# Attention and rational FFN in fp32 halves: P times V head by head, with V high and V low side by side in the stationary tile

## The chip, the cores and the metric

The kernel runs on one core of one Trainium2 chip. The metric is the device time of one execution in microseconds (us); lower is better. The core has a matrix engine (TensorE, PE in the profile; PEld is its loading of stationary tiles), three engines for elementwise work (VectorE or DVE, ScalarE or ACT, GpSimd or POOL) and a queue from which all DMAs here are issued (SyncE or SP). PE writes to PSUM, eight banks of 128 partitions by 512 fp32 columns; POOL does not read PSUM in this kernel.

## The reference

Block-causal attention over 8 batches and 8 heads of 576 positions by 64, and then a feed-forward net (FFN) on the 4608 tokens, whose nonlinearity is a rational function:

```python
scores = scale * np.matmul(q, k.transpose(0, 1, 3, 2))
mask = (pos[:, None] // 64) >= (pos[None, :] // 64)
scores = np.where(mask, scores, -1000000000.0)
attn = np.exp(scores - np.max(scores, axis=-1, keepdims=True))
attn = attn / (np.sum(attn, axis=-1, keepdims=True) + 1e-09)
x = np.matmul(attn, v)          # then heads side by side: (4608, 512)
...
h = x @ w_in                    # (4608, 2048)
P = a[0] + a[1] * h + a[2] * h**2 + a[3] * h**3
Q = 1.0 + np.abs(b[0]) * np.abs(h) + np.abs(b[1]) * h**2
return (P / (Q + 1e-06)) @ w_out   # (4608, 512)
```

## The kernel before, in words

**Halves.** Matmuls run on fp32r operands. Each fp32 operand x is split into a high part (a cast to fp32r) and a low part (x minus the high part). A product is the sum of three matmuls: low times high, high times high, high times low.

**Attention.** The work goes by pairs of heads: 32 pairs (8 batches by 4), each called p. `load` brings Q, K and V in by DMA. `prep` transposes Q and K on PE into a PSUM bank (L410); ACT writes the high part (L414) and DVE the low part (L417); DMAs then lay high and low parts of one head below each other in 128 partitions. `scores` goes over five query tiles t (64, 128, 128, 128, 128 queries; 64 to 576 keys) and two heads j: two matmuls (L509, L510), a row maximum on DVE (L517, L521), exp with row sums on ACT (L525), normalisation on POOL (L539, L545), transposes of P on PE (L566), and again a high part on ACT (L581) and a low part on DVE (L583). Transposed P lies in `pt0`, `pt1`, `pt2`, one set for all pairs.

**P times V.** `vprep` splits V into `vpad`: per head and for the first block apart, four ACT casts (L453) and four POOL subtractions (L455). `vpad` holds the two heads' columns in such places, among zeros, that a 128-column window (`vblock`) gives an output with head 0 in partitions 0 to 63 and head 1 in 64 to 127, where one head's keys meet zeros of the other. `pv(p, g)` has two groups: g = 0 for the first three query tiles (5 key blocks, up to 320 columns) and g = 1 for the last two (9 blocks, 256 columns). Each block takes three matmuls (L604), so 15 and 27 per pair; all sum up in one bank. ACT writes the high part of the result (L617), DVE the low part (L619), and a DMA stores both in `xscr` (L622). The transposes of a pair wait for P times V of the pair before.

**FFN.** Chunks of 256 tokens (18 of them). Early units (`ffn0`: four units of two 128-wide columns of `w_in`, chunks 0 to 14) run beside attention: 24 matmuls of 256 columns (L741), the nonlinearity `wide` on ACT, POOL and DVE (L678 to L703), 12 matmuls of 512 columns (L760). All else is late (`ffn1`, chunks of 512 tokens, L855 and L881, 12 and 12 matmuls of 512 columns per unit; L858 where only one half of a chunk is left): 84 units. It starts when attention has given its memory back (`switch`).

**Order.** The kernel records every step as an operation with an engine, a modelled cost, a priority and its dependencies. `Plan.order` then goes through a modelled time: whenever an engine is free it takes the ready operation of the lowest `pri`, binds buffers and banks, and adds a LATENCY of the consuming engine to each dependency. What it gives out is the program order; each engine runs its queue in that order and waits on semaphores. Pools of empty slots are quotas on the eight banks: QA (6) for attention, QH (2) for the early FFN's h, QO (2) for its output.

## Time and profile before

| | before |
|---|---|
| median of 3 runs (lowest to highest) | 1280.77 us (1278.71 to 1282.59) |
| the profiled execution | 1278.76 us |
| its span, first to last instruction | 1276.6 us |
| busy: PE, PEld, DVE, ACT, POOL | 96%, 85%, 74%, 70%, 66% |
| P times V, first and last start (L604) | 29.8 and 792.5 us |
| first early FFN matmul (L741), first late one (L855) | 101.6 and 803.7 us |

In the slices of the page each digit is the busy share of a fortieth of the span, in tenths. A group's row gives its line, engine and operation, out<-in by name, the shape and the count, then the busy time in us, the mean in ns of one, and the idle time of the engine just before with what ended it. Matmuls overlap: a single one of 256 columns is shown 0.28 us long, while the next starts 0.12 us later, so stretches of the chain give their price better than their own length. In the rows of the waits stand who waited for whom, the sum in us, how often, and the longest.

### The profile page before, as it was taken

How to read it: one execution, taken by the hardware profiler on the slowest of the kernel's cores; microseconds unless marked ns; L12 is line 12 of the kernel's file. 1: busy time of each engine (PE TensorE's matmuls, PEld its weight loads, DVE VectorE, ACT ScalarE, POOL GpSimd, SP SyncE). 2: the span in 40 equal slices, each digit the busy share in tenths (PEclk: the TensorE clock that was granted, in tenths of full speed). 3: DMA queues.
4: the chain of work that ended last, by engine and by line, in shares of the span. 5: the costliest groups of instructions: out<-in, count | busy, mean ns of one | idle time of the engine just before them, and what ended most of it. 6: DMA issues, size and time to landing. Idle time of an engine off the chain costs nothing.

```text
span 1276.6 us, 23262 instructions
## 1 busy us (share of the span) xinstructions
PE 1230.6 (96%) x7560; PEld 1088.4 (85%) x7560; DVE 942.3 (74%) x1916; ACT 891.4 (70%) x2230; POOL 848.5 (66%) x1218
## 2 busy tenths in 40 slices
PE   7879999999999999999999999999999999999997
PEld 5669799899998999999988999888888888888885
DVE  7867887778787777778876876666676777677664
ACT  6778787778877788787787886555655555555554
POOL 6757876767767767676767776566665666665564
PEclk8989999999999999999999999999999999999999
DMA  5888876678777857786696741911142233224110
GB/s 147 217 235 213 221 191 174 179 191 210 192 194 185 225 162 200 180 212 187 165 236 181 196 133 63 379 47 41 59 132 67 89 109 118 81 66 132 34 33 33
DMA packets 222615, 195.12 MB, mean 153 GB/s; under 512 B 129312, under 2 KB 183584, under 8 KB 222496
## 3 DMA queue, kind: packets, MB, share of 16 engines
q1 hardware_dynamic: 222496, 193.65, 55.5%
q8 instruction: 60, 0.98, 0.3%
q14 instruction: 59, 0.48, 0.1%
HBM read 95.95 MB, written 44.56 MB: 110 GB/s over the span
## 4 chain that ended last, share of the span: by engine, by line
PE 68%; DVE 7%; DMA 7%; ACT 7%; POOL 6%; issue 3%; SPq 1%; POOLq 0%; ACTq 0%; DVEq 0%
PE psd L855 4%; PE psf L855 4%; PE psb L881 4%; PE psh L881 4%; PE pse L881 3%; PE psg L881 3%; PE psf L604 3%; DMA osa<-in_moe_w_in_dram 3%; PE psc L881 2%; PE psa L881 2%; PE psa L855 2%; PE psc L855 2%; PE psc L760 2%; PE psg L855 1%; PE psa L741 1%
## 5 line engine op out<-in xcount | busy, mean ns | idle before, releaser
L681 POOL TENSOR_SCALAR va<-ub,bab 128x512 f32<-128x512 f32 x60 | 46.8, 780 | 93.0 <-ACT ub L678 91.1
L681 POOL TENSOR_SCALAR vb<-ua,bab 128x512 f32<-128x512 f32 x57 | 44.2, 776 | 91.8 <-ACT ua L678 91.7
L703 POOL TENSOR_TENSOR glb<-sa,ghb 128x512 fp32r<-128x512 f32 x58 | 75.5, 1302 | 20.1 <-ACT ghb L702 17.7
L683 POOL TENSOR_TENSOR ub<-va,ub 128x512 f32<-128x512 f32 x60 | 77.9, 1299 | 4.6
L703 POOL TENSOR_TENSOR gla<-sb,gha 128x512 fp32r<-128x512 f32 x58 | 75.6, 1303 | 7.8 <-ACT gha L702 7.7
L455 POOL TENSOR_TENSOR vpl<-vra,vph 128x256 fp32r<-128x256 f32 (+1 forms) x128 | 67.8, 539 | 19.5 <-ACT vph L453 11.6
L683 POOL TENSOR_TENSOR ua<-vb,ua 128x512 f32<-128x512 f32 x57 | 74.0, 1298 | 4.6
L689 ACT ACTIVATE va<-ub,qcb 128x512 f32<-128x512 f32 x60 | 43.6, 727 | 46.0 <-POOL ub L683 45.8
L689 ACT ACTIVATE vb<-ua,qcb 128x512 f32<-128x512 f32 x57 | 41.3, 724 | 43.0 <-POOL ua L683 43.0
L702 ACT CAST ghb<-sa 128x512 fp32r<-128x512 f32 x58 | 36.1, 622 | 26.8 <-DVE sa L699 26.7
L702 ACT CAST gha<-sb 128x512 fp32r<-128x512 f32 x58 | 36.2, 624 | 11.1 <-DVE sb L699 10.9
L453 ACT CAST vph<-vra 128x256 fp32r<-128x256 f32 (+1 forms) x128 | 39.1, 324 | 1.8 <-POOL vph L323 0.4
L695 DVE SCALAR_TENSOR_TENSOR ub<-ub,psf 128x512 f32<-128x512 f32 x23 | 15.8, 686 | 25.5 <-ACT psf L693 25.4
L695 DVE SCALAR_TENSOR_TENSOR ub<-ub,psd 128x512 f32<-128x512 f32 x21 | 14.4, 687 | 26.5 <-ACT psd L693 26.3
L741 PE MATMUL psa<-x,wiha 128*128 128x256 f32 x176 | 33.2, 288 | 0.5 <-DVE sb L699 0.4
L741 PE MATMUL psf<-x,wiha 128*128 128x256 f32 x176 | 32.8, 285 | 0.5 <-DMA x<-xscr 0.5
L678 ACT ACTIVATE ua<-psf 128x512 f32<-128x512 f32 x25 | 15.0, 598 | 25.3 <-PE psf L855 21.1
L678 ACT ACTIVATE ua<-psd 128x512 f32<-128x512 f32 x24 | 14.3, 598 | 21.7 <-PE psd L855 19.4
L703 POOL TENSOR_TENSOR glb<-sb,ghb 128x512 fp32r<-128x512 f32 x14 | 18.1, 1296 | 16.1 <-ACT ghb L702 16.1
L741 PEld LDWEIGHTS psa<-x,wiha 128*128 128x128 f32 x176 | 27.3, 191 | 1.1 <-DVE sb L699 0.6
L741 PEld LDWEIGHTS psf<-x,wiha 128*128 128x128 f32 x176 | 27.5, 191 | 0.7 <-DMA x<-xscr 0.7
L741 PE MATMUL psb<-x,wiha 128*128 128x256 f32 x144 | 27.0, 286 | 0.0
(1662 smaller groups left out, 5599.0 us busy)
## 6 DMA issues: line engine op xcount, KB each, us to landing
xscr<-xsa SPq DMA_DIRECT2D x32, 320.0 KB, 2.9
x<-xscr SPq DMA_DIRECT2D x40, 256.0 KB, 4.5
qra<-in_q_dram SPq DMA_DIRECT2D x64, 144.0 KB, 3.7
qra<-in_k_dram SPq DMA_DIRECT2D x60, 144.0 KB, 2.9
vra<-in_v_dram SPq DMA_DIRECT2D x64, 128.0 KB, 2.5
xscr<-xsa SPq DMA_DIRECT2D x32, 256.0 KB, 3.7
ppa<-pscr SPq DMA_DIRECT2D x15, 512.0 KB, 4.0
osa<-in_moe_w_in_dram SPq DMA_DIRECT2D x10, 512.0 KB, 5.2
```

What stands on the lines that cost most here:

```text
L453: aop("ACT", (0.833 * n + 110, 0.833 * n + 200), lambda vh=vh, src=src: nc.scalar.copy(out=vh, in_=src()), rd=rd, wr=[("v", i, 0)], pri=pr ...
L455: aop("POOL", pool(n, True), lambda vh=vh, vl=vl, src=src: nc.gpsimd.tensor_tensor(out=vl, in0=src(), in1=vh.bitcast(F32), op=ALU.subtract ...
L604: nc.tensor.matmul(bank.t[:, s0:w], lhsT=vblock(vv, x), rhs=pp, start=(x == 0 and i == 0), stop=(x == nb - 1 and i == 2))
L681: op("POOL", pool(512, False, 2), lambda: nc.gpsimd.tensor_scalar(out=vt.t, in0=ut.t, scalar1=b1, scalar2=b0, op0=ALU.mult, op1=ALU.add), ...
L683: op("POOL", pool(512, True), lambda: nc.gpsimd.tensor_tensor(out=ut.t, in0=vt.t, in1=ut.t, op=ALU.mult), rd=[vt], wr=[ut], pri=pri)
L689: op("ACT", act(512, False, 1), lambda: nc.scalar.activation(out=vt.t, in_=ut.t, func=AF.Ln, bias=qcb), rd=[ut, "qcb"], wr=[vt], pri=pri)
L695: op("DVE", dve(512), lambda: nc.vector.scalar_tensor_tensor(out=ut.t, in0=ut.t, scalar=QC, in1=r0.t, op0=ALU.add, op1=ALU.mult), rd=rk, w ...
L702: op("ACT", act(512, False), lambda: nc.scalar.copy(out=gh.t, in_=st.t), rd=[st], wr=[gh], pri=pri)
L703: op("POOL", pool(512, True), lambda: nc.gpsimd.tensor_tensor(out=gl.t, in0=st.t, in1=gh.t.bitcast(F32), op=ALU.subtract), rd=[st, gh], wr ...
L741: nc.tensor.matmul(h.t[:, j * CT:(j + 1) * CT], lhsT=w[:, dc, fs], rhs=xb[dc // 2].t[:, dc % 2, hl, :], start=(dc == 0 and i == 0), stop=( ...
L855: nc.tensor.matmul(h.t, lhsT=w[:, dc, fs], rhs=x.t[:, dc, hl, :], start=(dc == 0 and i == 0), stop=(dc == 3 and i == 2))
L881: nc.tensor.matmul(o[m].t, lhsT=g.t[:, c0:c0 + 128], rhs=w[:, ff, :], start=(a and i == 0 and j == 0), stop=(z and i == 2))
```

## The change

**P times V.** V's split tile is now `VP`, 10 blocks of 128 columns: in each, V high in columns 0 to 63 and V low in 64 to 127. The first key block of the two heads has a block each (0 and 9), with zeros in the other 64 partitions, which the loaded tile brings along: it is filled with zeros there once, and the two small V loads go to blocks 0 and 9. `vprep` splits everything with one ACT cast and one POOL subtraction of 640 columns.

`pv` goes head by head. For head j it takes block 0 (or 9) and every second block after it, two matmuls each (P low and P high against the same stationary tile). The bank then has the product with V high in partitions 0 to 63 and that with V low in 64 to 127. ACT copies the lower part out to the head's 64 partitions of a new tile `xf`, DVE adds the upper part to it. When both heads are there, ACT casts `xf` to the high part and POOL (before: DVE) subtracts the low one. In group 0 each head has its own bank, in group 1 both share one.

**Order.** LATENCY is 90 for PE (250) and 80 for ACT (40); ACT and DVE work on attention's banks has 2 taken off its priority number (15); QH is 3 (2); scores and prep leave 2 banks of the quota free (1); loads come 9 earlier in priority, `vprep` 3 later; `gate` lets early FFN and weight loads 20 ahead (12); the split of the late weights begins at 90 (110); early FFN covers chunks 0 to 13, and chunk 14 goes to the late part, which then has 88 units.

```diff
-LATENCY = {"PE": 250, "ACT": 40,
+LATENCY = {"PE": 90, "ACT": 80,
...
-            o.pri -= 15
+            o.pri -= 2
...
-    QA, QH, QO, QH1, QO1, QR1, QR = (Pool([None] * n) for n in (6, 2, 2, 2, 4, 2, 1))
+    QA, QH, QO, QH1, QO1, QR1, QR = (Pool([None] * n) for n in (6, 3, 2, 2, 4, 2, 1))
...
-    def gate(pri, ahead=12):
+    def gate(pri, ahead=20):
...
-        pri = 10 * p - 12 + 0
+        pri = 10 * p - 12 + -9
...
-        pri = 10 * p + 3
...
+        pri = 10 * p + 6
+        vp = s["vp"] = Buf(VP)
+        aop("ACT", (0.833 * 640 + 110, 0.833 * 640 + 200), lambda: nc.scalar.copy(out=vp.t[:, :, 0:D], in_=vr.t),
+            rd=[(vr, j, i) for j in range(2) for i in range(2)], wr=[(vp, 0)], pri=pri)
+        aop("POOL", pool(640, True), lambda: nc.gpsimd.tensor_tensor(
+            out=vp.t[:, :, D:2 * D], in0=vr.t, in1=vp.t[:, :, 0:D].bitcast(F32), op=ALU.subtract),
...
-                for i, (vv, pp) in enumerate(((vh, lo), (vh, hi), (vl, hi))):
-                    nc.tensor.matmul(bank.t[:, s0:w], lhsT=vblock(vv, x), rhs=pp,
-                                     start=(x == 0 and i == 0), stop=(x == nb - 1 and i == 2))
...
+        xf = Buf(XF)
+        whole = Buf(banks, QA) if g else None
+        for j in range(2):
+            bank, at = (whole, 256 * j) if g else (Buf(banks, QA), 0)
...
+                xs_ = (0, *range(1 + j, nb, 2))
...
+                    for i, pp in enumerate((lo, hi)):
+                        nc.tensor.matmul(bank.t[:, at + s0:at + w], lhsT=vp.t[:, x or 9 * j], rhs=pp,
+                                         start=(x == 0 and i == 0), stop=(x == xs_[-1] and i == 1))
...
+            aop("ACT", act(w), lambda bank=bank, at=at, j=j: nc.scalar.copy(
+                out=xf.t[64 * j:64 * j + 64, :w], in_=bank.t[64:128, at:at + w]), rd=[(bank, j)], wr=[(xf, j)], pri=pri)
+            aop("DVE", dve(w), lambda bank=bank, at=at, j=j: nc.vector.tensor_tensor(
+                out=xf.t[64 * j:64 * j + 64, :w], in0=bank.t[0:64, at:at + w], in1=xf.t[64 * j:64 * j + 64, :w],
+                op=ALU.add), rd=[(bank, j)], wr=[(xf, j)], pri=pri)
...
-        aop("ACT", act(w), lambda: nc.scalar.copy(out=xs.t[:, 0, :w], in_=bank.t[:, :w]),
-            rd=[bank], wr=[(xs, 0)], pri=pri)
-        aop("DVE", dve(w), lambda: nc.vector.tensor_tensor(
-            out=xs.t[:, 1, :w], in0=bank.t[:, :w], in1=xs.t[:, 0, :w].bitcast(F32), op=ALU.subtract),
+        aop("ACT", act(w, False), lambda: nc.scalar.copy(out=xs.t[:, 0, :w], in_=xf.t[:, :w]),
+            rd=[(xf, 0), (xf, 1)], wr=[(xs, 0)], pri=pri)
+        aop("POOL", pool(w, True), lambda: nc.gpsimd.tensor_tensor(
+            out=xs.t[:, 1, :w], in0=xf.t[:, :w], in1=xs.t[:, 0, :w].bitcast(F32), op=ALU.subtract),
...
-    split_weights(wscr, NFA, NFB, [110 + 220 * i / NPLB for i in range(NPLB)], True)
+    split_weights(wscr, NFA, NFB, [90 + 220 * i / NPLB for i in range(NPLB)], True)
...
-    U0 = [list(range(EARLY[c] if c < len(EARLY) else 4 if c < NCH - 3 else 0)) for c in range(NCH)]
+    U0 = [list(range(EARLY[c] if c < len(EARLY) else 4 if c < NCH - 4 else 0)) for c in range(NCH)]
```

What this makes of the queues, at two places. On PE, the beginning of a first group of P times V in the middle of attention, before (psg is the bank, pt0 and pt1 are transposed P high and low, vph and vpl V high and low; L604 is the matmul):

```order
L604 MATMUL psg<-pt0l,vph 128x320
L604 MATMUL psg<-pt0h,vph 128x320
L604 MATMUL psg<-pt0h,vpl 128x320
L604 MATMUL psg<-pt1l,vph 128x256
L604 MATMUL psg<-pt1h,vph 128x256
L604 MATMUL psg<-pt1h,vpl 128x256
```

The same place on PE now (vpa holds V high and low; the line is L606), both heads:

```order
L606 MATMUL pse<-pt0l,vpa 128x320
L606 MATMUL pse<-pt0h,vpa 128x320
L606 MATMUL pse<-pt1l,vpa 128x256
L606 MATMUL pse<-pt1h,vpa 128x256
...
L606 MATMUL psd<-pt0l,vpa 128x320
L606 MATMUL psd<-pt0h,vpa 128x320
L606 MATMUL psd<-pt1l,vpa 128x256
L606 MATMUL psd<-pt1h,vpa 128x256
```

Two matmuls stand per block where three stood, for two or three blocks of each head, and the second head's follow at once in another bank. On ACT, what follows a second group of P times V, before (xsa is the result in halves, vra the loaded V):

```order
L617 CAST xsa<-psa 128x256
L453 CAST vph<-vra 64x64 x2
L525 ACTIVATE p2a,sme<-psh,nme 128x320
L453 CAST vph<-vra 128x4x64 x2
L702 CAST ghb<-sa 128x512
```

The same place on ACT now (xfa is the joined tile, psg the bank of both heads):

```order
L612 COPY xfa<-psg 64x256
L694 ACTIVATE psb<-vb 128x512
L612 COPY xfa<-psg 64x256
L417 ACTIVATE hl1a<-psf 128x288
L417 ACTIVATE hl1a<-psc 128x288
L449 CAST vpa<-vra 128x10x64
L680 ACTIVATE sa<-psd,ncoef 128x512
L618 CAST xsa<-xfa 128x256
L573 CAST pt0h<-psc 128x64
L573 CAST pt0h<-psg 128x128
```

One cast out of the bank has become two copies with an FFN step between them; the four V casts have become one; a cast of the joined tile comes seven rows after the first copy, ahead of casts that empty transposed P.

## The prediction

> **What bounds the kernel now.** I read the page first, then the busy times by stage, then what PE (TensorE) waits for, then the chain of waits, and last the groups of the lines that are edited.

> The page's first two parts, with the chain's shares by engine:

> ```profile
> span 1276.6 us, 23262 instructions
> PE 1230.6 (96%) x7560; PEld 1088.4 (85%) x7560; DVE 942.3 (74%) x1916; ACT 891.4 (70%) x2230; POOL 848.5 (66%) x1218
> PE   7879999999999999999999999999999999999997
> PEclk8989999999999999999999999999999999999999
> PE 68%; DVE 7%; DMA 7%; ACT 7%; POOL 6%; issue 3%; SPq 1%; POOLq 0%; ACTq 0%; DVEq 0%
> ```

> PE is full except in the first slices, and 68% of the chain runs on it. A share over the whole span hides stages, so here is each stage: the start up to the first matmul of the early FFN, the stretch in which attention and early FFN are mixed, a remnant, and the late FFN. The last two rows are a part of the mixed stretch.

> ```profile
> core 0: us, PE busy (x) PEld busy (x) DVE busy (x) ACT busy (x) POOL busy (x), PEclk, DMA share, GB/s
> 0.00:101.00 101.00, 78.21 (x496) 64.92 (x497) 74.36 (x194) 68.76 (x223) 64.60 (x126) 0.88 0.79 203
> 101.00:795.00 694.00, 678.59 (x4926) 630.93 (x4925) 544.34 (x1261) 549.71 (x1568) 495.77 (x833) 1.00 0.71 186
> 804.00:1276.00 472.00, 464.79 (x2089) 384.53 (x2087) 317.42 (x454) 268.08 (x431) 282.94 (x255) 1.00 0.28 91
> 650.00:700.00 50.00, 48.01 (x351) 44.62 (x350) 36.94 (x89) 39.49 (x115) 36.05 (x62) 1.00 0.80 204
> 700.00:750.00 50.00, 50.00 (x376) 47.42 (x374) 41.31 (x95) 41.93 (x120) 36.46 (x62) 1.00 0.73 197
> ```

> The mixed stretch holds 28 of the 32 head pairs and leaves PE idle for only 694 - 678.6 = 15.4 us, while ACT is busy 549.7/694 = 79.2%, DVE 78.4%, POOL 71.4%. In 700 to 750 us PE never idles, and ACT (83.9%) and DVE (82.6%) are busier than elsewhere: they go faster when PE does. So matmul time taken out of this stretch should come off the end. In the first 101 us (4 pairs) PE is busy only 77% and no matmul saved there counts. What PE waits for in the mixed stretch, the largest rows:

> ```profile
> PE psc L509 <- DVE pt2l L583: 1.2, 3, 0.6
> PE psf L410 <- DMA qra<-in_k_dram: 1.1, 1, 1.1
> PE psb L566 <- DVE pt0l L583: 1.0, 1, 1.0
> ```

> No single wait is over 1.2 us in total: there is no other engine that PE stands behind as a rule.

> **The change part by part.** First the matmuls. Rows of the chain (start, length, how many matmuls) price them:

> ```profile
> 421.78 1.88 PE pse L604 x15
> 434.55 3.23 PE psa L604 x27
> 438.18 0.69 PE psh L760 x3
> 440.36 2.87 PE psd L741 x24
> 1000.39 2.72 PE psf L855 x12
> 1005.83 2.72 PE psa L855 x12
> 1196.76 2.87 PE psf L858 x24
> ```

> A matmul of 256 columns takes 3.23/27 = 0.120 us. The 15 of the first group are 12 of these and three of 320 columns: (1.88 - 12 x 0.120)/3 = 0.148 us. A pair costs 1.88 + 3.23 = 5.11 us now. Afterwards each head takes 2 matmuls for each of its own key blocks: 4 of 320 and 8 of 256 columns for the first group (1.55 us), 20 of 256 for the second (2.39 us), 3.94 us together. That is 1.17 us less per pair, **32.8 us** for the 28 pairs of the mixed stretch. For the 4 pairs of the start I count nothing; the bounds there are 4.7 us gained (if PE did set the pace) and 4.4 us lost (if ACT's 1.09 us per pair, below, did). I take the middle because PE, ACT and DVE are all at 68 to 77% there.

> Chunk 14 of the FFN goes from early to late. Its 4 early units cost 2.87 + 4 x 0.69 = 5.63 us each, 22.5 us; chunk 15 alone cost 4 half-width late units of 2.87 + 2.72 = 5.59 us, 22.4 us; both together are now 8 full-width units of 1005.83 - 1000.39 = 5.44 us, 43.5 us. Net **-1.4 us**, with 22.5 us leaving the mixed stretch and 21.1 us added to the late one, where PE is the bound.

> Then the work that is added on the other engines. Prices by shape:

> ```profile
> L453 ACT CAST vph<-vra 128x256 fp32r<-128x256 f32 x64 | 23.5, 404 | 0.6
> L453 ACT CAST vph<-vra 64x64 fp32r<-64x64 f32 x64 | 15.7, 245 | 1.2 <-POOL vph L323 0.4
> L617 ACT CAST xsa<-psf 128x256 fp32r<-128x256 f32 x10 | 3.8, 375 | 4.6 <-issue 4.2 <-PE psf L604 0.3
> L617 ACT CAST xsa<-psf 128x320 fp32r<-128x320 f32 x6 | 2.6, 428 | 1.5 <-PE psf L604 1.5
> L619 DVE TENSOR_TENSOR xsa<-psf,xsa 128x256 fp32r<-128x256 f32 x10 | 4.2, 419 | 4.4 <-ACT xsa L617 4.4
> L619 DVE TENSOR_TENSOR xsa<-psf,xsa 128x320 fp32r<-128x320 f32 x6 | 2.9, 485 | 1.5 <-ACT xsa L617 1.5
> L455 POOL TENSOR_TENSOR vpl<-vra,vph 128x256 fp32r<-128x256 f32 x64 | 47.1, 756 | 4.6 <-POOL vpl L455 1.6 <-ACT vph L453 0.4
> L455 POOL TENSOR_TENSOR vpl<-vra,vph 64x64 fp32r<-64x64 f32 x64 | 20.6, 322 | 14.9 <-ACT vph L453 11.2 <-POOL vpl L455 1.4
> L703 POOL TENSOR_TENSOR gla<-sb,gha 128x512 fp32r<-128x512 f32 x58 | 75.6, 1303 | 7.8 <-ACT gha L702 7.7
> ```

> ACT, per pair. The V cast is one of 640 columns in place of 2 x 0.245 + 2 x 0.404 = 1.30; by the slope from 64 to 256 columns (0.83 ns each) it is 0.72, so -0.58. Four copies out of PSUM stand in place of two casts: +0.80. Two casts of the joined tile are new: 0.404 and, by the slope, 0.457. Sum +1.09 us. DVE has four adds for two subtractions: +0.90 us. POOL had 2.16 us of V splits; now one of 640 columns (by the slope from 256 to 512, 1.58 us) and two new subtractions (0.756 and 0.893): +1.07 us. A copy from partitions 64 to 127 into 0 to 63 stands in no row; I take the price of the same columns without a shift, between that and twice it.

> Over the 28 pairs ACT gets 30.5, DVE 25.3, POOL 30.0 us more; the 4 units that leave take 268.1/84 = 3.2, 3.8 and 3.4 us each with them (84 late units in the row from 804 us). If the stretch shrank by all of 32.8 + 22.5 us to 638.7 us, ACT would be busy (549.7 + 30.5 - 12.8)/638.7 = 88.8%, DVE 86.8%, POOL 80.2%. All this lies beside PE, but its cover gets thin: ACT's free share falls from 20.8 to 11.2%. **Stalls** are the unknown term. From below: zero more, by the row from 700 us, where PE idles not at all with ACT at 83.9%. From above: +78 us, if ACT cannot go beyond its present 79.2% (567.4/0.792 = 716 us). If PE's 15.4 us grow as ACT's free share shrinks, they become 28.6, +13. I take **+10**, nearest to the row from 700 us.

> DVE may pay more than the four adds. Rows of its timeline (start, length):

> ```profile
> 7.78 0.55 DVE L362 CAST kqba<-p4a 64x576 fp32r<-64x576 f32 x1
> 8.35 0.55 DVE L362 CAST kqbb<-p4a 64x576 fp32r<-64x576 f32 x1
> 8.82 0.43 DVE L417 SCALAR_TENSOR_TENSOR hl0a<-psa,hl0a 128x288 fp32r<-128x288 f32 x1
> 9.18 0.44 DVE L417 SCALAR_TENSOR_TENSOR hl0a<-psb,hl0a 128x288 fp32r<-128x288 f32 x1
> ```

> The L417 pair overlaps by 0.07 us; the L362 casts, which write the upper and the lower 64 partitions in turn, leave no overlap between 7.78 and 8.35 us. The second head's add reads and writes the upper half of the joined tile, so it and its successor may each lose that overlap: 112 times 0.07 = 8 us of DVE in the stretch, 88% busy in place of 86.8%. [...]

> Edits with one answer. The order shows no wait inside a PE block of P times V. ACT's cast of the joined tile waits for DVE's second add; behind it on ACT stand the casts that empty transposed P, which PE waits for (0.4 us each time it is late; in the +10). The V load of the next pair now waits for one POOL step instead of four, with Q, K and store issues behind it on SP; DMA stays at 0.71. The two zero fills of the old V tiles leave POOL in the start, where it is 36% idle: nothing. At the end of attention the store's chain grows by an ACT cast and a POOL step, 0.404 + 0.756 = 1.2 us, and PE's remaining early FFN covers it: 36 matmuls of 256 columns and 36 of 512 now stand between the last P times V and the first late one (36 x 0.120 + 36 x 0.23 = 12.6 us), where 48 and 24 stood (11.3 us). The latencies, priorities, the third bank for early FFN and the earlier weight split only reorder; they go into the stall term with both signs.

> Sum: the profiled execution took 1278.76 us (span 1276.6 and 2.2 around it), 2.0 under the median of the three runs. 1278.8 - 32.8 - 1.4 + 10 = **1254.6, say 1255 us**.

> **The rivals.**

> *The bank becomes the wait (1276 us).* The first group now takes two of attention's six banks, the second keeps one until both halves have been copied and added. If each of the 56 groups held PE for one more ACT copy (0.375 us), 21 us come back. Against it: the P times V rows are not among PE's largest waits. Chance 14%.

> *ACT becomes the bound (1300 us), the slower side.* In the mixed stretch PE's transposes and P times V need ACT's exponentials and casts in order; 567.4 us of ACT work must fit. Break-even is a stretch of 694 - 21.1 = 672.9 us, ACT at 84.3%. If ACT stops halfway between 79.2 and 84.3%, the stretch lasts 694 us and the kernel 1278.8 + 21.1 = 1300; at 79.2% it is 1322. For it: ACT and DVE would be the busiest ever. Against it: 83.9% in the row from 700 us came with PE full, so PE, not ACT, set that pace. Chance 12%.

> *Nothing stalls (1240 us).* If the start's 4.7 us count as well and the third bank keeps PE supplied, 1278.8 - 32.8 - 4.7 - 1.4 = 1240. Chance 13%.

> That the matmuls stay is excluded: 1024 P times V matmuls stand in the order where 1344 stood.

> **How the numbers follow.** The forecast, with stalls of 0 to 20 us (1245 to 1265), has 57%; 4% are left for the reordered start going wrong by several microseconds. A difference of 0.3% (3.8 us) is about what a measurement of this kernel tells from none. Faster: the forecast, the case without stalls and 10 of the bank's 14, 80%. Slower: ACT's 12 and half of the rest, 14%. Same: 6%. The range from 1238 to 1282 leaves out the best half of the case without stalls and ACT as the bound.

> **What would show it.** Right: P times V groups of 1.55 and 2.39 us in the chain, the first late matmul at about 804 - 32.8 - 22.5 + 10 = 759 us, a late stage of some 493 us, ACT at 86 to 88% in the mixed stretch, PE idle there under 30 us. The rivals would show as waits of P times V for an ACT copy or DVE add (bank), or as PE idle over 50 us with ACT or DVE named (bound). Wrong altogether: a mixed stretch that is not shorter than 673 us.

## The result, and the profile after

The kernel after takes 1289.61 us (median of 6 runs, 1287.69 to 1291.98), the kernel before 1279.39 us beside it. The ratio is **1.008**, 95% interval 1.006 to 1.010: slower by 0.8%, some 10 us, where 1255 us was forecast. The profiled execution took 1290.01 us with a span of 1288.1, so the two spans (1276.6 and 1288.1) show the difference in full. The page after, its first two parts and the chain's shares by engine:

```profile
span 1288.1 us, 22392 instructions
PE 1216.2 (94%) x7144; PEld 1055.8 (82%) x7144; DVE 973.5 (76%) x1978; ACT 933.2 (72%) x2262; POOL 878.1 (68%) x1186
PE   6778899899999999999999999999999999999997
PEclk9879899999999999999999999999999999999999
PE 63%; DVE 10%; ACT 9%; POOL 7%; DMA 5%; issue 3%; SPq 1%; POOLq 0%; ACTq 0%; DVEq 0%
```

PE has 416 matmuls fewer and is busy 14 us less, yet the span is longer: its share in the chain falls from 68 to 63%, and ACT, DVE and POOL take what it gives up. By stage (start, mixed, late; then the two stretches that were shown of before):

```profile
core 0: us, PE busy (x) PEld busy (x) DVE busy (x) ACT busy (x) POOL busy (x), PEclk, DMA share, GB/s
0.00:111.60 111.60, 82.38 (x481) 67.42 (x482) 84.73 (x216) 79.17 (x238) 73.18 (x130) 0.85 0.82 195
111.60:796.00 684.40, 650.13 (x4540) 590.29 (x4540) 564.02 (x1296) 573.36 (x1574) 510.56 (x792) 0.99 0.72 188
796.00:1288.10 492.10, 483.68 (x2126) 398.03 (x2125) 324.76 (x468) 280.62 (x451) 294.35 (x265) 1.00 0.27 87
650.00:700.00 50.00, 47.10 (x324) 42.13 (x324) 42.05 (x100) 43.57 (x124) 37.18 (x61) 1.00 0.79 202
700.00:750.00 50.00, 48.50 (x351) 44.49 (x351) 40.64 (x98) 42.10 (x123) 37.45 (x63) 1.00 0.65 172
```

The mixed stretch lasts 684.4 us (702.1 before, first early-FFN matmul at 101.7 us to first late one at 803.8) and PE idles in it for 34.3 us where it idled 15.4. The prices are as forecast. Rows of the chain (start, length, matmuls), a first group's two heads and the second group of another pair:

```profile
390.30 0.76 PE pse L606 x6
391.06 0.83 PE psc L606 x6
399.34 2.39 PE pse L606 x20
```

1.59 and 2.39 us, where 1.88 and 3.23 stood. One more figure is used from here on, the **lost time** of a stretch: its length less what its matmuls take at PE's own pace, start to start with no wait and full clock (0.120 us for 256 columns, 0.147 for 320, 0.203 for 448, 0.227 for 512, 0.108 for a transposition, and so on for each shape in the trace). It sees short gaps too, which a modelled end of a matmul covers in the busy column. A part of it is the clock: busy time by (1 - granted clock), summed over twelve equal parts of the stretch.

| profiled execution | start, own pace + lost | mixed, own pace + lost (of it clock) | late, own pace + lost |
|---|---|---|---|
| before | 53.4 + 48.3 | 667.4 + 34.8 (0) | 463.7 + 9.0 |
| after | 51.0 + 60.8 | 612.5 + 72.0 (8) | 482.1 + 9.7 |
| difference | -2.4 + 12.5 | -54.9 + 37.2 | +18.4 + 0.7 |

So the matmuls that were to leave did leave (54.9 us of the mixed stretch, of which 18.4 come back in the late one), and 37 us of loss in the mixed stretch and 12 in the start ate more than that. What PE waits for there, largest rows:

```profile
engine line waited for: us in total, times, longest us
PE psd L606 <- ACT p4a L517: 1.9, 1, 1.9
PE psd L558 <- POOL pkb L531: 1.7, 2, 1.1
PE psf L742 <- DVE pt0l L575: 1.4, 1, 1.4
PE psg L761 <- POOL gla L704: 1.4, 1, 1.4
PE psf L761 <- POOL glb L704: 1.4, 1, 1.4
PE psa L742 <- DVE xfa L614: 1.2, 1, 1.2
```

No row is large, as before the change: many waits of about a microsecond, on each of the three engines and in nearly every kind of PE's work. Two places show how such waits arise. The first, from the timeline by engine (start, length; rows of other work are left out), at 127 to 134 us:

```profile
127.34 0.66 ACT L636 ACTIVATE ua<-osa 128x512 f32<-128x512 f32 x1 [1.30 <-DMA osa<-in_moe_w_in_dram]
129.23 1.56 POOL L451 TENSOR_TENSOR vpa<-vra,vpa 128x640 fp32r<-128x640 f32 x1 [2.37 <-ACT vpa L449]
129.70 0.19 ACT L517 ACTIVATION_READ_ACCUMULATOR p2a<-pse,nmd 128x1 f32 x1
130.74 0.72 POOL L620 TENSOR_TENSOR xsa<-xfa,xsa 128x256 fp32r<-128x256 f32 x1
131.56 0.21 POOL L527 TENSOR_SCALAR rcd<-smd 128x2 f32<-128x2 f32 x1
131.58 0.74 DVE L688 SCALAR_TENSOR_TENSOR sb<-sb,coef,psg 128x512 f32<-128x512 f32 x1
132.60 0.15 DVE L529 RECIPROCAL rcd<-rcd 128x2 f32<-128x2 f32 x1
132.84 0.40 POOL L531 TENSOR_TENSOR pkb<-p2a,rcd 128x128 f32<-128x128 f32 x1 [0.50 <-DVE rcd L529]
133.30 0.48 PE L558 MATMUL psh<-ident,pkb 128*128 128x128 f32 x1 [1.05 <-POOL pkb L531]
```

The row sums are ready at 129.89 us. POOL's step of 0.21 us on them stands in its queue behind the V subtraction in one step and the new subtraction of the joined tile, and starts 1.67 us later; DVE's reciprocal then stands behind an FFN step and a maximum; POOL normalises at 132.84, and PE's transpose waits 1.05 us. The new steps don't begin this by themselves: ACT first stood 1.30 us for the DMA of a weight (L636, a step that the kernel before has too), the copy of the second head and the V cast came behind it, and POOL had waited 2.37 us for that cast. The second place, at 321 to 323 us:

```profile
321.23 0.72 ACT L449 CAST vpa<-vra 128x640 fp32r<-128x640 f32 x1
321.96 0.37 ACT L612 COPY xfa<-psa 64x256 f32<-64x256 f32 x1
322.85 0.42 DVE L614 TENSOR_TENSOR xfa<-psa,xfa 64x256 f32<-64x256 f32 x1
323.32 0.50 PE L742 MATMUL psa<-x,wiha 128*128 128x256 f32 x2 [1.18 <-DVE xfa L614]
```

ACT copies the second head's half only after the V cast, DVE adds it later still, and the early FFN waits 1.18 us for that bank. Both are in-order queues in which a new step stands ahead of one that PE waits for. At the first place the granted clock falls as well:

```profile
126.00:130.00 4.00, 3.83 (x29) 3.57 (x28) 2.45 (x8) 2.52 (x7) 1.64 (x2) 1.00 1.07 219
130.00:134.00 4.00, 1.84 (x8) 1.04 (x7) 3.97 (x10) 3.77 (x12) 3.05 (x7) 0.89 0.28 66
134.00:138.00 4.00, 4.00 (x20) 3.79 (x20) 3.80 (x10) 3.80 (x13) 3.26 (x7) 0.50 0.30 91
```

After two waits of 1.1 us in four microseconds (the other ended with DVE's L700, a step of the early FFN's nonlinearity that gave its bank back) the granted clock is 0.50 for the next four. Such dips are the 8 us of clock in the table; in the kernel before the granted clock was 1.00 over the whole mixed stretch.

### The profile page after: what moved, and what is told of

The parts are those of the page before. It is cut to its first block, busy times and chain, and to the rows that moved or that the text cites. A ratio compares the mean times of both kernels' runs of the same rounds, so it can differ in the third digit from the quotient of the medians.

```text
span 1288.1 us, 22392 instructions
## 1 busy us (share of the span) xinstructions
PE 1216.2 (94%) x7144; PEld 1055.8 (82%) x7144; DVE 973.5 (76%) x1978; ACT 933.2 (72%) x2262; POOL 878.1 (68%) x1186
## 4 chain that ended last, share of the span: by engine, by line
PE 63%; DVE 10%; ACT 9%; POOL 7%; DMA 5%; issue 3%; SPq 1%; POOLq 0%; ACTq 0%; DVEq 0%
PE psh L856 4%; PE psb L882 3%; PE psf L856 3%; PE pse L882 3%; PE psc L882 3%; PE psg L856 3%; PE psd L882 2%; PE psd L856 2%; PE psa L856 2%; PE psg L882 2%; PE psa L882 2%; PE psc L856 1%; PE psh L606 1%; DMA osa<-in_moe_w_out_dram 1%; PE psg L761 1%
## 5 line engine op out<-in xcount | busy, mean ns | idle before, releaser
L704 POOL TENSOR_TENSOR glb<-sa,ghb 128x512 fp32r<-128x512 f32 x60 | 77.7, 1295 | 54.5 <-ACT ghb L703 54.3
L682 POOL TENSOR_SCALAR vb<-ua,bab 128x512 f32<-128x512 f32 x56 | 43.1, 770 | 55.6 <-ACT ua L679 55.3
L451 POOL TENSOR_TENSOR vpa<-vra,vpa 128x640 fp32r<-128x640 f32 x32 | 50.0, 1562 | 26.9 <-ACT vpa L449 20.6
L620 POOL TENSOR_TENSOR xsa<-xfa,xsa 128x320 fp32r<-128x320 f32 x64 | 53.8, 840 | 15.7 <-ACT xsa L618 11.3
L703 ACT CAST ghb<-sa 128x512 fp32r<-128x512 f32 x60 | 37.2, 621 | 34.0 <-DVE sa L700 33.8
L703 ACT CAST gha<-sb 128x512 fp32r<-128x512 f32 x59 | 36.6, 621 | 29.2 <-DVE sb L700 27.3
L618 ACT CAST xsa<-xfa 128x320 fp32r<-128x320 f32 x64 | 27.6, 431 | 3.1 <-DVE xfa L614 2.3
L742 PE MATMUL psf<-x,wila 128*128 128x256 f32 x104 | 29.4, 282 | 0.0
L696 DVE SCALAR_TENSOR_TENSOR ua<-ua,psf 128x512 f32<-128x512 f32 x21 | 14.4, 685 | 17.9 <-ACT psf L694 17.9
L742 PE MATMUL psc<-x,wiha 128*128 128x256 f32 x144 | 27.5, 289 | 0.0
L679 ACT ACTIVATE ub<-psf 128x512 f32<-128x512 f32 x23 | 13.8, 600 | 14.8 <-PE psf L856 13.5
L742 PE MATMUL psd<-x,wiha 128*128 128x256 f32 x128 | 24.2, 287 | 0.0
L449 ACT CAST vpa<-vra 128x640 fp32r<-128x640 f32 x32 | 23.2, 726 | 1.3 <-PE psa L606 0.8
L742 PEld LDWEIGHTS psc<-x,wiha 128*128 128x128 f32 x144 | 22.8, 194 | 0.3 <-DVE pt2l L575 0.2
```

Of the source, the lines that this page charges most:

```text
L449: aop("ACT", (0.833 * 640 + 110, 0.833 * 640 + 200), lambda: nc.scalar.copy(out=vp.t[:, :, 0:D], in_=vr.t), rd=[(vr, j, i) for j in range( ...
L451: aop("POOL", pool(640, True), lambda: nc.gpsimd.tensor_tensor(out=vp.t[:, :, D:2 * D], in0=vr.t, in1=vp.t[:, :, 0:D].bitcast(F32), op=ALU ...
L618: aop("ACT", act(w, False), lambda: nc.scalar.copy(out=xs.t[:, 0, :w], in_=xf.t[:, :w]), rd=[(xf, 0), (xf, 1)], wr=[(xs, 0)], pri=pri)
L620: aop("POOL", pool(w, True), lambda: nc.gpsimd.tensor_tensor(out=xs.t[:, 1, :w], in0=xf.t[:, :w], in1=xs.t[:, 0, :w].bitcast(F32), op=ALU. ...
L682: op("POOL", pool(512, False, 2), lambda: nc.gpsimd.tensor_scalar(out=vt.t, in0=ut.t, scalar1=b1, scalar2=b0, op0=ALU.mult, op1=ALU.add), ...
L703: op("ACT", act(512, False), lambda: nc.scalar.copy(out=gh.t, in_=st.t), rd=[st], wr=[gh], pri=pri)
```

## The experiments

Two theories stood at first. **Load** (L): the work added on ACT, DVE and POOL makes PE wait, whatever the order. **Order** (O): the planner's new constants cost what the matmuls gain. Later ones concern single steps of the new form (V in one step, banks, pieces of PE work). Each run is given with its ratio to the kernel before, timed beside it; differences between runs are differences of these ratios by 1280 us. "Mixed lost" is the lost time of the mixed stretch, in its profiled execution; for the low part on DVE that execution was 7.6 us under the median, for one piece 5.3 us over it.

| run | median us | ratio (95%) | start | mixed | mixed lost (clock) |
|---|---|---|---|---|---|
| after | 1289.6 | 1.008 (1.006, 1.010) | 111.8 | 684.5 | 72 (8) |
| old constants | 1317.8 | 1.028 (1.024, 1.032) | 123.3 | 720.9 | 91 (6) |
| old P·V, new constants | 1287.4 | 1.0045 (1.002, 1.0065) | 109.3 | 681.0 | 35 (0) |
| old eviction | 1275.5 | 0.995 (0.993, 0.997) | 114.3 | 668.3 | 57 (2) |
| more matmuls | 1326.8 | 1.035 (1.031, 1.039) | 115.9 | 716.1 | 68 (4) |
| V in four | 1302.6 | 1.0155 (1.0135, 1.017) | 111.5 | 697.4 | 85 (11) |
| low part on DVE | 1315.2 | 1.028 (1.024, 1.032) | 104.0 | 711.6 | 94 (7) |
| side work, free | 1304.5 | 1.018 (1.0155, 1.020) | 123.7 | 687.6 | 42 (6) |
| latency 100 | 1297.4 | 1.011 (1.0095, 1.013) | 110.5 | 695.4 | 80 (10) |
| side work behind P·V | 1305.1 | 1.021 (1.017, 1.024) | 110.8 | 698.8 | 54 (8) |
| seven banks | 1306.8 | 1.021 (1.019, 1.022) | 111.6 | 700.2 | 90 (2) |
| seven banks, two joined tiles | 1304.8 | 1.020 (1.018, 1.022) | 111.8 | 699.0 | 89 (2) |
| loads late | 1309.3 | 1.023 (1.021, 1.024) | 113.4 | 698.2 | 84 (8) |
| before, latency 260 | 1280.5 | 0.999 (0.998, 1.000) | 101.6 | 704.2 | 37 (2) |
| old eviction, more matmuls | 1306.3 | 1.019 (1.017, 1.020) | 114.6 | 697.3 | 52 (2) |
| side work, ACT | 1298.7 | 1.014 (1.012, 1.015) | 112.2 | 688.3 | 44 (6) |
| side work, DVE and POOL | 1313.7 | 1.0245 (1.022, 1.027) | 111.1 | 710.6 | 63 (8) |
| old P·V, two pieces | 1295.4 | 1.011 (1.009, 1.013) | 111.7 | 690.8 | 45 (2) |
| one piece | 1302.6 | 1.017 (1.013, 1.021) | 109.0 | 706.5 | 89 (18) |

**Old constants.** The kernel after with all order constants of before:

```diff
-LATENCY = {"PE": 90, "ACT": 80,
+LATENCY = {"PE": 250, "ACT": 40,
-            o.pri -= 2
+            o.pri -= 15
-    ... for n in (6, 3, 2, 2, 4, 2, 1))
+    ... for n in (6, 2, 2, 2, 4, 2, 1))
...  (gate 12, load +0, keep 1, vprep +3, weight split from 110, early chunks to NCH - 3)
```

> The new P times V, V split and eviction, with all constants of the order as before (latencies, priorities, quotas, gate, early chunks). Theory L (the added ACT, DVE and POOL work makes PE stall): 1280 to 1295 us, near the changed kernel's 1290. Theory O (the new order's constants lose the time): 1255 us, the forecast's sum.

Measured 1317.8 us, 25 us slower than after: outside of both. The new constants don't eat the gain of the new form, they help it; alone they are not the cause. The start takes 123.3 us here.

**Old P times V, new constants.** The other half: the kernel before with the constants of after.

> The old P times V with the new constants of the order. Theory L: 1275 to 1285 us, as before. Theory O: 1310 to 1325 us (before plus the 35 us by which the changed kernel missed the forecast).

Measured 1287.4 us, 1.0045: 6 us slower than before, just above what theory L expected. The mixed row, with the busy columns as above:

```profile
109.30:790.30 681.00, 664.49 (x4835) 617.66 (x4834) 533.39 (x1244) 540.79 (x1553) 480.32 (x819) 1.00 0.71 188
```

It loses 35 us, what before loses. What the constants cost is in the start, 109.3 us in place of 101.7. That does not make them the cause of the longer start in the kernel after: the new form with the old constants starts in 123.3 us, with the new ones in 111.8, and with the new ones and one step moved to DVE (below) in 104.0. The start answers to the order as a whole, and what makes it 10 us longer is open.

**Old eviction.** The kernel after, but with one ACT cast and one DVE subtraction per group, as before, on the first head's bank alone. The second head's result and the sum of the halves are left out.

```diff
-            aop("ACT", act(w), lambda ...: nc.scalar.copy(out=xf.t[64 * j:64 * j + 64, :w], in_=bank.t[64:128, at:at + w]), ...)
-            aop("DVE", dve(w), lambda ...: nc.vector.tensor_tensor(out=xf.t[...], in0=bank.t[0:64, ...], in1=xf.t[...], op=ALU.add), ...)
...
+        aop("ACT", act(w), lambda: nc.scalar.copy(out=xs.t[:, 0, :w], in_=one.t[:, :w]), ...)
+        aop("DVE", dve(w), lambda: nc.vector.tensor_tensor(out=xs.t[:, 1, :w], in0=one.t[:, :w], ...), ...)
```

> The changed kernel with the old eviction: one ACT cast and one DVE subtraction of the first head's bank; the second head's result and the sum of the halves are left out. It keeps 32 matmuls per pair and drops 1.66 us of ACT, 0.90 of DVE and 1.65 of POOL work per pair. Theory L: 1245 to 1260 us. Theory O: 1280 to 1290 us, since the constants are still the new ones.

Measured 1275.5 us, 16 us under after (14 by the spans), 6 under before, and between what the two theories expected:

```profile
114.30:782.60 668.30, 638.84 (x4527) 584.16 (x4526) 534.32 (x1235) 522.34 (x1455) 466.52 (x729) 1.00 0.73 190
```

With the eviction's work gone, 57 us are still lost, where the old P times V loses 35 with more busy time on ACT and POOL. So the eviction is a part of the cause, and load on ACT and POOL is not the rest of it.

**More matmuls.** The kernel after with ten matmuls of 256 columns on a stationary tile of zeros added per pair.

```diff
+                    if x and not (g and x > 6):
+                        nc.tensor.matmul(bank.t[:, at + s0:at + w], lhsT=ZZ, rhs=hi, start=False, stop=False)
                     for i, pp in enumerate((lo, hi)):
```

> The changed kernel with ten more matmuls of 256 columns per pair against a stationary tile of zeros, so that P times V costs PE 42 matmuls per pair again and the result is the same. If PE still sets the pace of the mixed stretch (theory O): 1290 + 32 x 1.2 = 1328 us. If the other engines set it (theory L): 1290 to 1305 us, the matmuls fall into PE's stalls.

Measured 1326.8 us: 35 us over after by the ratios, 37 by the spans.

```profile
115.90:832.00 716.10, 682.25 (x4834) 622.77 (x4833) 564.51 (x1294) 576.92 (x1576) 511.98 (x793) 0.99 0.67 177
```

Matmul time counts nearly in full in this stretch. With a stretch of 716 us, ACT's share is 80.6% in place of 83.8 and DVE's 78.8 in place of 82.4; if a full engine made the pace, the lost time would have shrunk by the 35 us added. It went from 72 to 68. What PE loses per pair hardly moved when the engines' shares fell by some 3 points.

**V in four steps.**

```diff
-        aop("ACT", (0.833 * 640 + 110, ...), lambda: nc.scalar.copy(out=vp.t[:, :, 0:D], in_=vr.t), ...)
+        for x0, x1 in ((0, 3), (3, 6), (6, 8), (8, 10)):
+            aop("ACT", ..., lambda xs_=xs_: nc.scalar.copy(out=vp.t[:, xs_, 0:D], in_=vr.t[:, xs_]), ...)
+            aop("POOL", pool(n, True), ...)
```

> The kernel after with one thing changed: V is split in four steps (of 192, 192, 128 and 128 columns) instead of one of 640. Each ACT cast is then 0.2 to 0.35 us long instead of 0.73, each POOL subtraction 0.4 to 0.6 us instead of 1.56; the sums per pair grow by some 0.4 us on ACT and 0.5 us on POOL. If the long steps are what PE's transposes stand behind (POOL's normalising of P queued behind a 1.56 us step, ACT's casts of transposed P behind a 0.73 us one), 8 to 15 us come back: 1275 to 1282 us. If the load of the engines is what counts, it gets slower by 3 to 10 us: 1293 to 1300. If neither, 1286 to 1293.

Measured 1302.6 us, 10 us over after. POOL's groups by shape, here one row for each width:

```profile
L455 POOL TENSOR_TENSOR vpa<-vra,vpa 128x192 fp32r<-128x192 f32 x64 | 39.4, 625 | 19.4 <-ACT vpa L452 16.8 <-PE psc L610 2.0
L455 POOL TENSOR_TENSOR vpa<-vra,vpa 128x128 fp32r<-128x128 f32 x64 | 31.3, 502 | 0.4
```

The four steps cost POOL 2 x 0.625 + 2 x 0.502 = 2.25 us per pair instead of 1.56. The place at 129 us is real, but as short steps V gave nothing back. The run can't exclude a small gain, since it also puts 0.69 us per pair more on POOL and has another order.

**Low part of the first group on DVE.**

```diff
-        aop("POOL", pool(w, True), lambda: nc.gpsimd.tensor_tensor(
+        aop(("DVE", "POOL")[g], (dve(w), pool(w, True))[g], lambda: (nc.vector, nc.gpsimd)[g].tensor_tensor(
```

> The kernel after with the low part of the joined tile's first 320 columns subtracted on DVE instead of POOL: POOL gives up 0.93 us per pair, DVE gets about 0.49. If the queue of POOL is where the mixed stretch waits, it is faster by 4 to 10 us: 1280 to 1286. If DVE is the tighter one, slower by 3 to 10: 1293 to 1300.

Measured 1315.2 us, 25 us over after: the sign of "DVE is the tighter one", and more than its 10 us. But the step is not the 0.49 us that was counted. It has both inputs in SBUF; its mean is 0.61 us, and 8 of the 32 are longer, up to 1.44 us, where the same subtraction in the kernel before, with one input in PSUM, took 0.48 to 0.49 us each time. So the run doesn't tell a tight DVE from a step that became longer, nor from another order.

**Side work that waits for nothing**, on the old P times V in the new order.

```diff
+        for i in range(2):
+            aop("ACT", act(128, False), lambda: nc.scalar.copy(out=zz[0:32], in_=zz[0:32]), wr=[("zz", 0)], pri=pri, after=init_zz)
+        for i in range(2 - g):
+            aop("DVE", dve(128), lambda: nc.vector.tensor_tensor(out=zz[32:64], ..., op=ALU.add), ...)
+        aop("POOL", pool(128, True), lambda: nc.gpsimd.tensor_tensor(out=zz[64:96], ..., op=ALU.add), ...)
```

> The old P times V in the new order (1287.4 us), with work added that nothing waits for and that waits for nothing: per pair 4 ACT copies, 3 DVE adds and 2 POOL adds of 128 columns on 32 partitions, some 1.2, 0.85 and 0.93 us, about what the change adds. If load by itself makes PE stall, the mixed stretch loses what it lost from there to the kernel after, 30 to 37 us: 1315 to 1325. If the stalls of the kernel after come from the chain of its own steps (banks, joined tile, V in one step), the time stays at 1285 to 1297.

Inconclusive. With no dependency the planner put most of this work into the first microseconds, where engines were free: the start grew from 109 to 124 us and the mixed stretch got little of it.

**Side work behind P times V.** The same, with each piece after its pair's P times V (`after=init_zz + pvs[p, g]`).

> As the run before it with added side work on the old P times V in the new order, but each pair's added work now waits for that pair's P times V, so that it can't gather in the start: per pair 4 ACT copies, 3 DVE adds and 2 POOL adds of 128 columns on 32 partitions (1.2, 0.85, 0.93 us), which nothing waits for. If load by itself makes PE stall, the lost time of the mixed stretch goes from 35 to some 65 to 72 us and the time to 1317 to 1325. If the stalls of the kernel after come from its own chain of steps, the lost time stays under 45 us and the time at 1287 to 1300.

Measured 1305.1 us, 21 us over the run without it, and 54 us lost in place of 35: half way between the two expectations. Work that nothing waits for does come with lost time on PE, about half of what the change lost. It was not quite the work that was planned: per pair ACT's copies took 1.16 us, POOL's adds 0.82 and DVE's adds 1.40 us in place of 0.85, for a reason that the next runs show.

**Side work on ACT alone, on DVE and POOL alone.** The same lines, cut to one part each.

> The old P times V in the new order (1287.4 us) with four ACT copies of 128 columns added per pair (1.2 us) behind P times V, nothing on DVE or POOL. If ACT's load is what costs, as the rival with ACT as the bound had it, most of the 18 to 20 us of all the side work are there: 1299 to 1308. If not, 1285 to 1294.

> The old P times V in the new order with the DVE and POOL part of the side work alone (per pair 3 DVE adds, 0.85 us, and 2 POOL adds, 0.93 us). If DVE and POOL cost as much as ACT or more, 1297 to 1306. If ACT is the one, 1285 to 1294.

ACT's 1.2 us per pair cost 12 us, of which the mixed stretch lost 9, 6 of them clock. DVE's and POOL's parts cost 26 us, more than all three parts in one run (21 us):

```profile
112.20:800.50 688.30, 668.07 (x4824) 621.99 (x4825) 533.96 (x1240) 557.31 (x1657) 478.16 (x819) 0.99 0.71 188
```

```profile
111.10:821.70 710.60, 681.41 (x4835) 626.76 (x4834) 582.68 (x1328) 543.52 (x1550) 506.62 (x875) 0.99 0.69 182
```

The first row is ACT alone (PE idle 20.2 us, for 16.5 without side work; ACT at 81.0%), the second DVE and POOL alone (PE idle 29.2 us, ACT at 76.5%, DVE at 82.0%, POOL at 71.3%). These are the two engines between which the chain of row sums, reciprocal and normalisation goes back and forth ahead of each transposition; the stretch of before at 700 us was as full on DVE with PE never idle. But the run can't be read as a price of 1.78 us per pair on them. The groups of the added steps, and two of DVE's adds with the POOL step beside each:

```profile
L619 DVE TENSOR_TENSOR zz<-zz 32x128 f32<-32x128 f32 x96 | 47.4, 494 | 3.0
L621 POOL TENSOR_TENSOR zz<-zz 32x128 f32<-32x128 f32 x64 | 26.4, 412 | 5.2
326.77 1.30 POOL L710 TENSOR_TENSOR gla<-sa,gha 128x512 fp32r<-128x512 f32 x1
327.34 0.88 DVE L619 TENSOR_TENSOR zz<-zz 32x128 f32<-32x128 f32 x1
634.55 1.30 POOL L710 TENSOR_TENSOR glb<-sb,ghb 128x512 fp32r<-128x512 f32 x1 [0.27 <-ACT ghb L709]
634.70 1.29 DVE L619 TENSOR_TENSOR zz<-zz 32x128 f32<-32x128 f32 x1
```

An add that takes 0.28 us at its shortest takes 0.49 in the mean and up to 2.13. The two shown, with both inputs in SBUF, end 0.15 and 0.14 us after the POOL step that was running beside them. The three adds of a pair take DVE 1.48 us (3 x 0.494) in place of the 0.85 that was planned. The new adds of the kernel after, with one input in PSUM, took 0.41 to 0.42 us for each of the 64 with 256 columns, and 24 of those lay wholly inside one POOL step. By the measured lengths, 37.1 us of work on ACT cost 12 us and 73.8 us on DVE and POOL cost 26: about the same per microsecond. That a part cost more than the whole says how far such runs scatter. Which engine counts most is not shown.

**Latency 100.** One constant of the kernel after, `"PE": 90` to 100, to see what an order costs by itself.

> The kernel after with the planner's latency for PE at 100 instead of 90: the same instructions, in an order that differs in small things all over. It measures how far the time scatters from order alone: every theory expects 1286 to 1293 if the order's small things cancel. If it lies further off, differences of that size between other kernels prove nothing about their edits.

Measured 1.0114, 4 us over after and just outside: 80 us lost in the mixed stretch. The same instructions in another order, so differences below some 5 us between kernels of this form say nothing about an edit, and the next runs show that it can be more.

**Seven banks; seven banks and a joined tile per group; loads late.**

```diff
-    QA, QH, QO, QH1, QO1, QR1, QR = (Pool([None] * n) for n in (6, 3, 2, 2, 4, 2, 1))
+    QA, QH, QO, QH1, QO1, QR1, QR = (Pool([None] * n) for n in (7, 3, 2, 2, 4, 2, 1))
```

```diff
-    XF = tiles(att, 1, [128, 320], F32, "xf")
+    XF = [tiles(att, 1, [128, w], F32, f"xf{w}") for w in (320, 256)]
...
-        xf = Buf(XF)
+        xf = Buf(XF[g])
```

```diff
-        pri = 10 * p - 12 + -9
+        pri = 10 * p - 12 + 0
```

> The kernel after with seven PSUM banks instead of six for attention at a time. If the two banks of the first group of P times V and the bank held through copies and adds are what the mixed stretch waits for, 10 to 25 us come back: 1265 to 1280. If banks aren't it, 1284 to 1298, which is the scatter that a small change of the order showed.

> The run with seven banks, and a joined tile for each of the two groups, so that the copies of a group need not wait for POOL's subtraction of the one before. If the single joined tile holds the banks, it is faster than with seven banks alone by 5 to 15 us. If neither banks nor the joined tile matter, 1284 to 1298.

> The kernel after with the due time of the Q, K and V loads as it was (9 later, in tenths of a pair). If the earlier loads are what makes the start longer with the new constants (102 us before, 109 to 112 with them), the start is 102 to 105 us and the time 1280 to 1284. If not, the start stays at 109 to 113 us and the time at 1285 to 1298.

All three are 15 to 19 us slower than after, with 84 to 90 us lost in the mixed stretch. More banks and a second joined tile give nothing back, and the second tile differs from the banks alone by 1 us, in the same order of PE's matmuls: the single joined tile is not what PE waits for there. The earlier loads aren't what makes the start longer (113 us without them). The banks and the loads also shift the whole order, which may hide a gain.

**Before, latency 260.** The same step on the kernel before.

> The kernel before with the planner's latency for PE at 260 instead of 250: the same instructions in an order that differs in small things. If an order from constants that were not chosen for it costs 4 to 20 us in either form, as the same kind of step cost in the kernel after, 1284 to 1300. If the old form is robust and only the new one is tight, 1276 to 1284.

Measured 1280.5 us, ratio 0.999 with an interval from 0.998 to 1.000: no change. But the step hardly made another order: matched by the traces, 99.9% of PE's matmuls of the mixed stretch stand in the order of the kernel before, where latency 100 left 46% of them in the order of the kernel after. So this run says nothing of how the old form bears another order. The run with old P times V and all the new constants does, 28% in the order of before: it lost 35 us too and was 6 us slower. Every one of the six kernels with the new form's steps and a shifted order (old constants, latency 100, seven banks with and without tiles, loads late, one piece) was slower than after, by 4 to 25 us. The kernel after is thus the fastest order on record of its form, and a run that edits it pays for the lost order too.

**Old eviction, more matmuls.** The run with the old eviction (with what it leaves out), with the ten matmuls of zeros per pair as well.

> The run with the old eviction (1275.5 us; second head's result and sum of halves left out) with ten matmuls of zeros added per pair, so that P times V is as long as before. If the shorter P times V is what uncovers PE's 57 us of lost time, they fall to 35 to 45 and the time grows by only 20 to 27 us, to 1295 to 1303. If the lost time belongs to working head by head, it stays at 52 to 62 and the time grows by the full 36 to 38 us: 1311 to 1314.

Measured 1306.3 us, 31 us more, and 52 lost in place of 57: between the two. At most 6 us of the loss come from P times V being shorter and covering less.

**Old P times V in two pieces; new P times V in one piece.**

```diff
+        more = None if g else Buf(banks, QA)
+        for j in range(2):
+            pvs[p, g].append(aop("PE", ..., lambda j=j: mms(j), rd=keys + vk,
+                                 wr=[(bank, j)] + ([(more, j)] if more and j else []), pri=pri, after=pvs[p, g][:j]))
```

```diff
-            pvs[p, g].append(aop("PE", (n1[0] + rest[0], n1[0] + rest[1]), mms, ..., wr=[(bank, j)], pri=pri))
+        pvs[p, g].append(aop("PE", (n1[0] + rest[0], n1[0] + rest[1]), mms2, ..., wr=[(both[0][0], 0), (both[1][0], 1)], pri=pri))
```

> The old P times V in the new order (1287.4 us) with its matmuls in two pieces that the planner places apart, first the first head's blocks, then the second's, into the same bank, and a second bank held, unused, for the first group. If pieces and bank are what costs the new form its last 16 us, the lost time of the mixed stretch goes from 35 to 45 to 55 us and the time to 1297 to 1307. If they cost nothing, 1284 to 1294.

> The kernel after with both heads' matmuls of a group as one piece of PE work, the eviction unchanged. If the two pieces cost, 8 to 16 us come back: 1274 to 1283. If not, 1286 to 1306, where the kernels lie whose order was shifted a little.

In the old form two pieces and a second bank cost 8 us. The lost time, 45 in place of 35, is at the low end of what was expected if they cost; the time lies between the two expectations. Taken back in the new form they return nothing: 1302.6 us, 11 over after, 18 of its 89 us lost to the clock. So this is not settled: the first run is compatible with a part of the 16 us, the second with none, and both are within what a shifted order does.

No version of the new form that computes everything came out under the kernel before.

## Why the prediction was wrong, point by point

- **What bounds the kernel: right.** PE does set the pace of the mixed stretch; added matmul time came out at the end nearly in full (37 of 38 us expected), ACT at 80.6%.
- **P times V and chunk 14: right in size.** 54.9 us left the mixed stretch (55.3 forecast), the late stage lasts 492 us (493 forecast).
- **The added work: right on ACT**: the 554.4 us of the whole mixed stretch before (702.1 us of it) + 30.5 - 12.8 make 572.1, and 573.4 were measured. By the same sum it is near on DVE (564.0 for 560.4) and POOL (510.6 for 517.2).
- **The stall term: the step that failed.** It was +10, "nearest to the row from 700 us". It measured +37, of which about 8 are the clock. The row from 700 us showed that PE can stay full with ACT at 83.9%, not that it does so with other steps in the queues: over the whole mixed stretch of the kernel after ACT is at 83.8% and PE idles 34.3 us. The share of an engine was the wrong measure, in the forecast and in the bounds (the scaling of PE's 15.4 us by ACT's free share gave +13). With the old eviction ACT is at 78.2% and DVE at 80.0%, and 57 us are lost; the old P times V in the same order loses 35 at 79.4 and 78.3%. What counts in its place is, by the two places above, where the new steps stand in each in-order queue; that is read from the timelines, and no run isolates it.
- **"I count nothing" for the start: failed.** It is 10 us longer, outside of the bounds of 4.7 gained and 4.4 lost. 8 of the 10 appear with the new constants alone, but the new form alone makes it 22 us longer, and one run with both, and one step moved to DVE, only 2. So the order moves the start by more than the bounds allowed, and "the latencies, priorities, ... only reorder; they go into the stall term with both signs" left it no room there; the text gave 4% to a start that goes wrong. The cause of these 10 us stays open.
- **The rivals.** *ACT becomes the bound* gave the right sign, and the time of the case lay near (1300 us for 1290), but that is luck, since its mechanism is not the one: with ACT's share lower by 3 points the loss stayed. *The bank becomes the wait* is seen at 321 us, but of the 80 us by which matmuls of the stretch start late, a copy or add (L612, L614) ends only 6, and a seventh bank gave nothing in a kernel with another order. *Nothing stalls* fell.
- **The overlap that DVE's adds lose: seen in the trace.** The forecast put 8 us of DVE time on it in the stretch; had PE waited for all of it, it still could not make up for the 27 us that were missing in the stall term. Around the adds of both heads of a group, in DVE's timeline:

```profile
128.43 0.42 DVE L614 TENSOR_TENSOR xfa<-psb,xfa 64x256 f32<-64x256 f32 x1 [1.48 <-ACT xfa L612]
128.77 0.47 DVE L513 TENSOR_REDUCE nmd<-pse 128x1 f32<-128x320 f32 x1
129.28 0.42 DVE L614 TENSOR_TENSOR xfa<-psb,xfa 64x256 f32<-64x256 f32 x1
129.72 0.62 DVE L513 TENSOR_REDUCE nme<-psh 128x1 f32<-128x448 f32 x1
```

The reduction behind the first head's add starts 0.08 us before that add ends; the second head's add overlaps neither its forerunner (end 129.24) nor its successor. Over the whole execution the next DVE step overlaps the first head's add by 0.07 to 0.08 us in 35 of 64 cases, and the second head's in 1 of 64.

- **What would show it.** By the forecast's own test the mixed stretch would last under 673 us; it lasts 684, PE idles in it for 34 us, not under 30, and the first late matmul comes at 796 us, not 759.

Where the 37 us come from, as far as the runs go: the eviction's work 14 to 16 us (run with the old eviction), the shorter cover of P times V up to 6, and some 16 are **open**. V in one step and the number of banks have no run that speaks for them; the two pieces of PE work have one for and one against. The parts need not add up, since each run also has another order, and an order by itself moved this form by 4 to 19 us.

## What to carry to other kernels

An engine's share of busy time says whether its work fits, not whether it comes in time. Where several in-order queues hand small steps to and fro, price each added step by what stands behind it in its queue and who waits for that, besides its own length. Work that nobody waited for still cost 12 us on ACT and 26 on DVE and POOL. If you load an engine on purpose to test it, read the length of the added steps in that run's own trace: here one third of DVE's grew, and the run measured something else than it was built for. And if an edit comes with another order, look at each stage for what the order alone does, the start as well, and try more than one order before a difference of a few microseconds is put down to the edit.

## What the runs showed of the hardware

```profile
153.63:157.05 3.42, 2.07 (x12) 1.61 (x13) 3.25 (x8) 2.92 (x9) 3.33 (x4) 1.00 0.86 252
320.89:324.30 3.41, 1.51 (x10) 1.12 (x10) 3.19 (x10) 3.00 (x9) 2.83 (x5) 1.00 1.06 256
361.85:365.26 3.41, 1.53 (x12) 1.33 (x11) 3.41 (x6) 1.32 (x4) 1.14 (x1) 1.00 0.00 0
225.32:228.73 3.41, 2.12 (x10) 1.84 (x11) 3.16 (x8) 3.34 (x10) 3.09 (x3) 1.00 1.11 246
```

PE was busy 61, 44 and 45% of the three, 38% of the one before 133 us, and 62% of the last. Cut in the same way, the mixed stretches of all twenty profiles have 48 steps at full clock with PE busy under 55%, and half the clock follows 39 of them; of the 3927 with 62% or more it follows 7 (in before and after alone 3 of 3 and 0 of 394). No wait of PE in the mixed stretch of the kernel after is over 1.9 us, and the clock halves there four times. It cost 8 us here and 18 in the run with one piece.

**DVE beside POOL.** Of the 96 adds with both inputs in SBUF in the run with DVE and POOL loaded, 34 took over 0.4 us where the shortest took 0.28, up to 2.13 us; the two shown above ended 0.15 and 0.14 us after a POOL step that ran beside them. The adds with one input in PSUM kept their length in the kernel after: 0.46 to 0.49 us for all 64 of 320 columns, 0.41 to 0.42 for all 64 of 256, though 20 and 24 of them lay wholly inside one POOL step.
